# All four block maxima of an attention head as masked maxima on VectorE

## The chip, the core and the metric

The kernel runs on one core of a Trainium2 chip. The metric is the device time of one execution in microseconds (us); before the change its median over three runs is 693.38 us (693.32 to 694.35). A core has five engines with a queue of instructions each, which wait for each other through semaphores: PE (TensorE; its weight loads appear as PEld), DVE (VectorE), ACT (ScalarE), POOL (GpSimd) and SP (SyncE, which issues most DMAs here).

## What is computed

Two independent results are put side by side. B is a 2D real Fourier transform of a 2048 x 576 array, a product with a spectral filter, and the inverse transform. A is attention in four segments of 512 positions with 32 heads of width 18, plus a linear memory that runs on from segment to segment. The change lies in A; cut to what matters:

```python
for s in range(N):                      # N = 4 segments, L = 512
    qs, ks, vs = q[:, :, s], k[:, :, s], v[:, :, s]
    logits = jnp.einsum("bhqd,bhkd->bhqk", qs, ks) * scale + mask   # mask: -1e9 above the diagonal
    p = _softmax(logits, axis=-1)
    a_dot = jnp.einsum("bhqk,bhkd->bhqd", p, vs)
    pq = phi(qs)
    num = jnp.einsum("bhld,bhde->bhle", pq, M)
    den = jnp.einsum("bhld,bhd->bhl", pq, z)[..., None] + 1e-6
    o = g * (num / den) + (1.0 - g) * a_dot
    ...
```

A softmax subtracts each row's maximum before the exponential. The kernel needs those row maxima ahead of the exponentials, and how it gets them is what changes.

## The kernel before

The kernel goes through these stages: the forward transform (to about 65 us), the projections of A with the middle of the transform beside them on VectorE (to about 278 us), the inverse transform with the first eleven heads' maxima between its matmuls (`prologue`, to about 349 us), attention (`attention`, to about 655 us), and the last output projection.

Attention counts heads and segments together: t runs over 128 pairs (segment, head), four of them make a group k. For each t there are two steps, eleven apart. `s1(t+11)` computes the scores with the query on the partitions, only to get the row maxima. `s2(t)` computes the scores again, with the key on the partitions and the maxima taken in as two more rows of the contraction, and ScalarE takes the exponential (L737, L742, L746). The product with the values (`pv`, L768) runs for two heads out of four, two blocks of keys at a time, so that it stands in every second t. Which of its instructions comes after which is written out by hand in `attention`: one part of `s1`, one of `s2`, three times over, with the value product ahead of the third; no scheduler reorders it.

The 512 queries of a head are four blocks of 128, numbered i = 0 to 3. Block i sees 128(i+1) keys, and only its last 128 keys touch the diagonal. `s1` makes three score tiles from one pool with three buffers (`ps1`, tag `s1`), which therefore go round once per head (a fourth kind of tile, the transposed maxima `mt`, takes one turn in every fourth head):

- the first tile holds block 2 (384 columns) and block 0 (128 columns). PE writes the scores (L687) and then adds, with a matmul of the identity `idb` on the triangle `tri` (L700), a large negative number above the diagonal. VectorE takes the maxima of the tile's four 128-wide pieces with a plain reduction (L701) into `mx`.
- the second holds block 3 (512 columns), the third block 1 (256 columns). VectorE adds the mask from `s.mask` and takes the maximum in one instruction, the masked maximum (L695, CUSTOM_DVE in the profile); an accumulator read (DVE_READ_ACCUMULATOR2) stores the result in `mg`. The masked scores themselves are discarded into `junk`, one buffer.
- for t = 11 to 14, the first heads of `attention`, the second and third tile also get the triangle on PE (L691) and a plain reduction (L692).

After four heads `mpath(k)` puts the maxima together: VectorE reduces the three pieces of block 2 (L713), ScalarE copies block 0 (L714), GpSimd splits the values in two bf16 parts (L716, L717), PE transposes them (L720), and a DMA writes them into the two extra rows of the queries.

From about 453 to 492 us and from 537 to 580 us the memory part of a segment (`combine` and `mem1`) runs between the heads, and in the stretches behind them its output projection (`oproj`, L916).

Of the kernel before, what the change touches and what calls it, by code (L numbers as in the profile page):

```python
# [5 lines left out]
F32=mybir.dt.float32; F32R=mybir.dt.float32r  # L6
# [81 lines left out]
class Pace:  # L88

    def __init__(s,total): s.left=total; s.acc=0.0; s.q=[]  # L90
# [275 lines left out]
BF=mybir.dt.bfloat16  # L366
# [43 lines left out]
class ATT:  # L410
    def __init__(s,nc,tc,io,cp,dp):
        s.nc,s.tc,s.io=nc,tc,io
        s.ident=cp.tile([128,128],F32,name="ident"); s.bm=cp.tile([126,7,19],F32,name="bm")
        s.tri=cp.tile([128,128],BF,name="tri"); s.idb=cp.tile([128,128],BF,name="idb")
        s.Mst=[None]+[cp.tile([126,5,126],F32,name=f"Mst{i}") for i in range(1,4)]
        s.zst=[None]+[cp.tile([126,5,32],F32,name=f"zst{i}") for i in range(1,4)]
        d=lambda n,sh,dt: dp.tile(sh,dt,name=n)
        s.qkD=[d(f"qkD{i}",[8,4,128,512],BF) for i in range(4)]
        s.reD=[d(f"reD{i}",[24,32,512],BF) for i in range(4)]
        s.pqD=[None]+[d(f"pqD{i}",[576,512],F32) for i in range(1,4)]  # L420
        s.vD=[d(f"vD{i}",[128,2448],F32) for i in range(4)]
        s.dp=dp
# [203 lines left out]
        return s.stack_dmas(0,0)+s.stack_dmas(0,1)  # L626
    def masks(s):
        nc=s.nc
        nc.scalar.copy(s.tri,s.mask[:,384:])
        nc.scalar.copy(s.idb,s.ident)  # L630
    def gates(s):
        nc=s.nc; e=s.bt
# [47 lines left out]
    def s1(s,t):  # L680

        nc=s.nc; k,hh=divmod(t,4); n,qd=divmod(k,2); h=4*qd+hh
        Q,K=s.Qs[n%3],s.Ks[n%4]; tp=s.sm
        assert (n,0) in s.loaded and (n,1) in s.loaded,(t,n)
        if hh==0: s.mg[k]=tp.tile([128,4,4],F32,name="mg"); s.mx[k]=tp.tile([128,4,4],F32,name="mx")
        def mm(out,i):
            nc.tensor.matmul(out,Q[:108,h,128*i:128*i+128],K[:108,h,:128*(i+1)],start=True,stop=True)  # L687
        def red(src,i):
            w=128*(i+1)
            if 11<=t<15:  # L690
                nc.tensor.matmul(src[:,w-128:w],s.idb,s.tri,start=False,stop=True,skip_group_check=True)  # L691
                nc.vector.tensor_reduce(out=s.mg[k][:,hh,i:i+1],in_=src,axis=mybir.AxisListType.X,op=OP.max)  # L692
                return
            junk=tp.tile([128,512],BF,name="junk",bufs=1)
            nc.vector.tensor_tensor_reduce(out=junk[:,:w],in0=src,in1=s.mask[:,512-w:],scale=1.0,scalar=-3.0e38,  # L695
                op0=OP.add,op1=OP.max,accum_out=s.mg[k][:,hh,i:i+1])
        pa=s.ps1.tile([128,512],F32,name="s1",tag="s1")
        for o,w,i in ((0,384,2),(384,128,0)):
            mm(pa[:,o:o+w],i)
            nc.tensor.matmul(pa[:,o+w-128:o+w],s.idb,s.tri,start=False,stop=True,skip_group_check=True)  # L700
        nc.vector.tensor_reduce(out=s.mx[k][:,hh],in_=pa.rearrange("p (b c) -> p b c",c=128),axis=mybir.AxisListType.X,op=OP.max)  # L701
        yield
        pc=s.ps1.tile([128,512],F32,name="s1",tag="s1")
        mm(pc,3); red(pc,3)
        yield
        pb=s.ps1.tile([128,256],F32,name="s1",tag="s1")
        mm(pb,1); red(pb,1)
        yield
    def mpath(s,k):

        nc=s.nc; n,qd=divmod(k,2); Q=s.Qs[n%3]
        mx=s.mx.pop(k); mg=s.mg.pop(k)
        nc.vector.tensor_reduce(out=mg[:,:,2:3],in_=mx[:,:,:3],axis=mybir.AxisListType.X,op=OP.max)  # L713
        nc.scalar.copy(mg[:,:,0:1],mx[:,:,3:])  # L714
        mh=s.mh; mg=mg.rearrange("p h i -> p (h i)")
        nc.gpsimd.tensor_copy(mh[:,0],mg)  # L716
        nc.gpsimd.tensor_tensor(mh[:,1],mg,mh[:,0],op=OP.subtract)  # L717
        yield
        pt=s.psm.tile([128,1024],BF,name="mt",tag=s.mtag)[:,:128]
        nc.tensor.transpose(pt,mh.rearrange("p a m -> p (a m)"),s.idb)  # L720
        yield
        mt=s.sm.tile([32,128],BF,name="mts",bufs=2)
        nc.scalar.copy(mt,pt[:32])
        out=Q[108:110,4*qd:4*qd+4].rearrange("p h (i c) -> p (h i) c",c=128)
        if s.now<0: nc.gpsimd.dma_start(out,mt)
        else: s.later(2,lambda: nc.scalar.dma_start(out,mt))
        yield
# [226 lines left out]
    def begin(s,sm,sp,ps1):  # L954
        s.late=[]; s.now=-1
        s.sm,s.sp,s.ps1=sm,sp,ps1
        s.mh=sm.tile([128,8,16],BF,name="mh",bufs=1); s.nc.gpsimd.memset(s.mh,0.0)
        s.mg={};s.mx={};s.m2={};s.P={};s.vs={};s.rc={};s.am={};s.pq={};s.ux={};s.rate=1.2;s.potag=s.rest=None
    def prologue(s):

        nc,io=s.nc,s.io
        yield
        s.load_v(0)
        q=s.stack_dmas(1,0)+s.stack_dmas(1,1)+s.stack_dmas(2,0)+s.stack_dmas(2,1)+[lambda: s.load_v(1)]+s.stack_dmas(3,1)
        for i in range(2): yield
        i=0
        for t in range(11):
            for _ in s.s1(t):
                for _ in range(1+(i%24==0)):
                    if q: q.pop(0)()  # L970
                i+=1
                yield
            if 2<=t<6: nc.gpsimd.dma_start(s.Ks[t-2][108:110].rearrange("p h c -> p (h c)"),io["neg1"])
            if t in (3,7): m=s.mpath(t//4); next(m)
            if t in (4,8): next(m); next(m,None)
        assert not q
# [221 lines left out]
```

## Time and profile before

| | |
|---|---|
| median of the runs | 693.38 us |
| lowest and highest of three | 693.32, 694.35 us |
| span of the profiled execution | 692.4 us |
| instructions in it | 14400 |
| granted TensorE clock | 9 tenths or more in all 40 slices |
| HBM read and written | 81.78 MB, 43.92 MB |
| masked maxima on VectorE (L695) | 248, 136.7 us busy |
| plain reductions (L701) | 128, 87.5 us busy |

The profile is one execution. Its span is 1.0 us below the median of the runs. A row of the timeline gives start, duration, engine, line, operation, what it writes and reads, and in brackets the idle time of the engine ahead of it with what ended it. Durations of neighbours on one engine overlap, since an instruction's time runs to its last write and the next one starts earlier; so what an instruction costs its engine is the distance from its start to the next start. The ends of matmuls are modelled. In the queries' names `x` and `x_...` stand for a buffer that is used in turn for several things (the first queries, the first keys and the mask lie in one).

### The profile page before, as it was taken

The numbers are of one execution on the slowest core, as the hardware profiler recorded it, in microseconds if no ns is written. First come the engines' busy times: TensorE is split into PE (matmuls) and PEld (weight loads), VectorE is DVE, ScalarE is ACT, GpSimd is POOL, SyncE is SP. The second block draws the span as 40 slices with busy tenths as digits, with TensorE's granted clock in tenths as the row PEclk, the third lists the DMA queues.
The fourth block names the chain that finished last, engine by engine and source line by source line (L and its number), as shares of the span: only waits on it lengthen the run. The fifth ranks groups of instructions, "written<-read, shape, count | busy, mean of one in ns | idle before, by whom it ended". The sixth has DMA issues, their size and how long they took to land.

```text
span 692.4 us, 14400 instructions
## 1 busy us (share of the span) xinstructions
PE 680.0 (98%) x5040; PEld 502.4 (73%) x5040; DVE 538.0 (78%) x1149; ACT 444.8 (64%) x997; POOL 191.6 (28%) x389
## 2 busy tenths in 40 slices
PE   9999999999999999999999999999999999999997
PEld 5999779879879879899955555445566455673497
DVE  5998989889789679688678888887755877557633
ACT  3876795675684483544468877787756877567531
POOL 2111000100200102656225433434323563235310
PEclk9999999999999999999999999999999999999999
DMA  9896475595486679798337775775756566322152
GB/s 340 288 306 187 141 199 186 172 297 175 145 241 191 196 206 323 187 296 243 100 106 193 203 206 156 202 198 135 162 160 174 151 173 164 122 81 97 28 167 78
DMA packets 76034, 127.60 MB, mean 184 GB/s; under 512 B 12812, under 2 KB 44202, under 8 KB 72370
## 3 DMA queue, kind: packets, MB, share of 16 engines
q1 hardware_dynamic: 69310, 110.67, 54.8%
q0 software_dynamic: 5632, 15.76, 7.9%
q8 instruction: 40, 0.66, 0.4%
q10 hardware_dynamic: 1020, 0.25, 0.2%
q14 instruction: 32, 0.26, 0.1%
HBM read 81.78 MB, written 43.92 MB: 182 GB/s over the span
## 4 chain that ended last, share of the span: by engine, by line
PE 87%; DMA 3%; ACT 3%; DVE 3%; issue 2%; POOL 1%; SPq 0%; ACTq 0%; DVEq 0%; POOLq 0%
PE pj L487 14%; PE pv L768 11%; PE s L687 11%; PE pjv L487 7%; PE po L916 7%; PE i L331 4%; PE i L320 4%; PE s L736 4%; PE f L145 4%; PE c L166 4%; PE s L740 3%; PE s L700 2%; PE po L945 2%; PE pn L843 2%; PE s L745 2%
## 5 line engine op out<-in xcount | busy, mean ns | idle before, releaser
L695 DVE CUSTOM_DVE_ANT_0 junk<-s,x 128x512 bf16<-128x512 f32 x248 | 136.7, 551 | 52.8 <-PE s L687 47.3
L750 POOL TENSOR_SCALAR_AFFINE_SELECT P<-P 128x512 f32<-128x512 f32 (+2 forms) x132 | 79.0, 623 | 71.2 <-ACT P L737 69.5
L701 DVE TENSOR_REDUCE mx<-s 128x4 f32<-128x512 f32 x128 | 87.5, 683 | 2.6 <-PE s L700 0.3
L768 PE MATMUL pv<-P,vs 128*32 128x512 f32 (+3 forms) x1024 | 82.2, 439 | 0.2 <-POOL P L750 0.2
L737 ACT ACTIVATE P<-s 128x512 f32<-128x512 f32 x128 | 77.7, 607 | 7.0 <-PE s L736 4.3
L742 ACT ACTIVATE P<-s 128x512 f32<-128x512 f32 x128 | 77.5, 605 | 2.6 <-PE s L741 2.3
L746 ACT ACTIVATE P<-s 128x256 f32<-128x256 f32 x128 | 49.9, 390 | 44.1 <-PE s L745 43.8
L687 PE MATMUL s<-Ks,Qs 108*128 108x384 bf16 (+3 forms) x256 | 69.2, 301 | 1.5 <-DMA vs<-vD 1.0
L768 PEld LDWEIGHTS pv<-P,vs 128*32 128x32 f32 x1024 | 26.8, 109 | 45.2 <-issue 35.5
L487 PE MATMUL pj<-x,wqkh 128*128 128x512 f32 x162 | 56.1, 408 | 0.0
L232 DVE TENSOR_TENSOR Z<-Z 128x580 f32<-128x580 f32 (+2 forms) x51 | 45.8, 912 | 0.6
L687 PEld LDWEIGHTS <-Qs 108*128 108x128 bf16 x320 | 31.5, 98 | 17.3 <-issue 7.1
L700 PE MATMUL s<-tri,idb 128*128 128x128 bf16 x256 | 43.0, 219 | 0.0
L548 POOL MEMSET vt<- 128x32 f32 x16 | 2.3, 162 | 139.2 <-PE pm L559 79.2
L320 PE MATMUL i<-civ,Y 128*128 128x256 f32 (+1 forms) x288 | 39.6, 289 | 0.9 <-POOL Y L305 0.9
L320 PEld LDWEIGHTS i<-civ,Y 128*128 128x128 f32 (+1 forms) x288 | 36.7, 181 | 1.9 <-POOL Y L305 1.3
L331 PE MATMUL i<-itab,T 128*128 128x290 f32 (+1 forms) x224 | 36.6, 306 | 0.1
L487 PE MATMUL pj<-xh,wqkl 128*128 128x512 f32 x90 | 35.6, 395 | 0.0
L487 PE MATMUL pj<-x,wqkl 128*128 128x512 f32 x90 | 35.5, 395 | 0.0
L487 PE MATMUL pj<-xh,wqkh 128*128 128x512 f32 x90 | 35.5, 395 | 0.0
L487 PEld LDWEIGHTS pj<-x,wqkh 128*128 128x128 f32 x162 | 30.5, 189 | 6.4
L687 PE MATMUL s<-Ks,x 108*128 108x384 bf16 (+3 forms) x128 | 34.6, 300 | 0.2
(216 smaller groups left out, 1792.5 us busy)
## 6 DMA issues: line engine op xcount, KB each, us to landing
qkD<-sp SPq DMA_DIRECT2D x32, 384.0 KB
xin<-xb SPq DMA_DIRECT2D x16, 384.0 KB
cfw<-cfw POOLq DMA_DIRECT2D x16, 384.0 KB, 5.0
civ<-civ POOLq DMA_DIRECT2D x16, 384.0 KB, 8.3
Ks<-qkD SPq DMA_DIRECT2D x12, 512.0 KB
x<-qkD SPq DMA_DIRECT2D x10, 512.0 KB
Qs<-qkD SPq DMA_DIRECT2D x10, 512.0 KB
vs<-vD SPq DMA_DIRECT2D x16, 310.5 KB
```

Source lines behind the costliest of these rows:

```text
L320: nc.tensor.matmul(p[:m,k],Y[i][:,q,c*128:c*128+m],cc[:,hl,o:o+256],start=n==0,stop=n==5)
L331: nc.tensor.matmul(p,x,t,start=n==0,stop=n==6)
L487: s.nc.tensor.matmul(out,a,b,start=i==0,stop=i==len(L)-1)
L687: nc.tensor.matmul(out,Q[:108,h,128*i:128*i+128],K[:108,h,:128*(i+1)],start=True,stop=True)
L695: nc.vector.tensor_tensor_reduce(out=junk[:,:w],in0=src,in1=s.mask[:,512-w:],scale=1.0,scalar=-3.0e38, op0=OP.add,op1=OP.max,accum_out=s.m ...
L700: nc.tensor.matmul(pa[:,o+w-128:o+w],s.idb,s.tri,start=False,stop=True,skip_group_check=True)
L701: nc.vector.tensor_reduce(out=s.mx[k][:,hh],in_=pa.rearrange("p (b c) -> p b c",c=128),axis=mybir.AxisListType.X,op=OP.max)
L737: nc.scalar.activation(P[0][:,hh],p0,AF.Exp,scale=SC)
L742: nc.scalar.activation(P[1][:,hh],p1,AF.Exp,scale=SC)
L746: nc.scalar.activation(P[2][:,hh],p2,AF.Exp,scale=SC)
L750: nc.gpsimd.affine_select(out=x[:,r],in_=x[:,r],pattern=[[0,r.stop-r.start],[1,128]],compare_op=OP.is_ge,fill=0.0,base=0,channel_multiplie ...
L768: nc.tensor.matmul(s.pvt[32*hh:32*hh+32,128*j:],vt[:,152*j+19*h:152*j+19*h+32],mv[0][:,hh,mv[1]],start=j==0,stop=j>1,skip_group_check=True)
```

## The change

All four block maxima of all heads become masked maxima on VectorE. The first tile still holds blocks 2 and 0, and now gets two masked maxima, 384 and 128 wide, which go straight into `mg`. The triangle, its matmuls on PE, the plain reductions, `mx`, and the two instructions of `mpath` that took `mx` apart are gone. The discarded scores go to one of two buffers: `junk512` for blocks 2 and 3, `junk256` for blocks 0 and 1, so that they alternate in the order 2, 0, 3, 1. The third tile is given 512 columns like the others and uses 256 of them.

```diff
-        s.tri=cp.tile([128,128],BF,name="tri"); s.idb=cp.tile([128,128],BF,name="idb")
+        s.idb=cp.tile([128,128],BF,name="idb")
...
     def masks(s):
         nc=s.nc
-        nc.scalar.copy(s.tri,s.mask[:,384:])
         nc.scalar.copy(s.idb,s.ident)
...
-        if hh==0: s.mg[k]=tp.tile([128,4,4],F32,name="mg"); s.mx[k]=tp.tile([128,4,4],F32,name="mx")
-        def mm(out,i):
-            nc.tensor.matmul(out,Q[:108,h,128*i:128*i+128],K[:108,h,:128*(i+1)],start=True,stop=True)
-        def red(src,i):
-            w=128*(i+1)
-            if 11<=t<15:
-                nc.tensor.matmul(src[:,w-128:w],s.idb,s.tri,start=False,stop=True,skip_group_check=True)
-                nc.vector.tensor_reduce(out=s.mg[k][:,hh,i:i+1],in_=src,axis=mybir.AxisListType.X,op=OP.max)
-                return
-            junk=tp.tile([128,512],BF,name="junk",bufs=1)
-            nc.vector.tensor_tensor_reduce(out=junk[:,:w],in0=src,in1=s.mask[:,512-w:],scale=1.0,scalar=-3.0e38,
-                op0=OP.add,op1=OP.max,accum_out=s.mg[k][:,hh,i:i+1])
-        pa=s.ps1.tile([128,512],F32,name="s1",tag="s1")
-        for o,w,i in ((0,384,2),(384,128,0)):
-            mm(pa[:,o:o+w],i)
-            nc.tensor.matmul(pa[:,o+w-128:o+w],s.idb,s.tri,start=False,stop=True,skip_group_check=True)
-        nc.vector.tensor_reduce(out=s.mx[k][:,hh],in_=pa.rearrange("p (b c) -> p b c",c=128),axis=mybir.AxisListType.X,op=OP.max)
-        yield
-        pc=s.ps1.tile([128,512],F32,name="s1",tag="s1")
-        mm(pc,3); red(pc,3)
-        yield
-        pb=s.ps1.tile([128,256],F32,name="s1",tag="s1")
-        mm(pb,1); red(pb,1)
-        yield
+        if hh==0: s.mg[k]=tp.tile([128,4,4],F32,name="mg")
+        def part(*J):
+            p=s.ps1.tile([128,512],F32,name="s1",tag="s1")
+            for o,i in J: nc.tensor.matmul(p[:,o:o+128*i+128],Q[:108,h,128*i:128*i+128],K[:108,h,:128*(i+1)],start=True,stop=True)
+            for o,i in J:
+                w=128*(i+1); b=256*(1+i//2); junk=tp.tile([128,b],BF,name=f"junk{b}",bufs=1)
+                nc.vector.tensor_tensor_reduce(out=junk[:,:w],in0=p[:,o:o+w],in1=s.mask[:,512-w:],scale=1.0,scalar=-3.0e38,
+                    op0=OP.add,op1=OP.max,accum_out=s.mg[k][:,hh,i:i+1])
+        part((0,2),(384,0))
+        yield
+        part((0,3))
+        yield
+        part((0,1))
+        yield
     def mpath(s,k):
 
         nc=s.nc; n,qd=divmod(k,2); Q=s.Qs[n%3]
-        mx=s.mx.pop(k); mg=s.mg.pop(k)
-        nc.vector.tensor_reduce(out=mg[:,:,2:3],in_=mx[:,:,:3],axis=mybir.AxisListType.X,op=OP.max)
-        nc.scalar.copy(mg[:,:,0:1],mx[:,:,3:])
-        mh=s.mh; mg=mg.rearrange("p h i -> p (h i)")
+        mh=s.mh; mg=s.mg.pop(k).rearrange("p h i -> p (h i)")
         nc.gpsimd.tensor_copy(mh[:,0],mg)
```

The order of instructions shows where they stand. On PE, in the head t = 19 of plain attention (the one whose times the prediction reads), from the third score tile of the head before to this head's first `s2` matmul, before the change; s_4550 is that third tile, s_4564 the head's first tile, Qs and Ks the queries and keys:

```order
L687 MATMUL s_4550<-Ks_3172,Qs_3170 128x256 [waits DVE_49]
L745 LDWEIGHTS x_2635
L745 MATMUL s_4554<-x_2635 128x256 [waits Activation_49]
L687 LDWEIGHTS Qs_3170
L687 MATMUL s_4564<-Ks_3172,Qs_3170 128x384 [waits DVE_49]
L700 LDWEIGHTS idb
L700 MATMUL s_4564<-tri,idb 128x128
L687 MATMUL s_4564<-Ks_3172,Qs_3170 128x128
L736 MATMUL s_4573<-Qs_3169,Ks_3171 128x512 [waits Activation_49]
```

And with the change, at the same place (s_4554 is now the third tile of the head before, s_4568 the first tile):

```order
L687 MATMUL s_4554<-Ks_3170,Qs_3168 128x256 [waits DVE_49]
L731 LDWEIGHTS x_2634
L731 MATMUL s_4558<-x_2634 128x256 [waits Activation_49]
L687 LDWEIGHTS Qs_3168
L687 MATMUL s_4568<-Ks_3170,Qs_3168 128x384 [waits DVE_49]
L687 MATMUL s_4568<-Ks_3170,Qs_3168 128x128
L722 MATMUL s_4578<-Qs_3167,Ks_3169 128x512 [waits Activation_49]
```

Four instructions are gone between the first tile and the `s2` matmul, two matmuls and two weight loads (the second pair, behind the 128-wide matmul, reads like the first). What the remaining ones wait for is the same: the first tile's matmul still waits for VectorE to give its buffer free.

On VectorE at the same place, from the masked maximum of the third tile of the head before to the end of this head, before the change (ISA is the masked maximum, and the row behind it, with mg alone, its accumulator read):

```order
L695 ISA junk,mg<-s_4550,x_2635 128x256 [waits DVE_49,PE_49]
L695 ISA mg 128x1
L701 TENSOR_REDUCE mx<-s_4564 128x4 [waits PE_49]
L695 ISA junk,mg<-s_4576,x_2635 128x512 [waits DVE_49,PE_49]
L695 ISA mg 128x1
L695 ISA junk,mg<-s_4585,x_2635 128x256 [waits DVE_49,PE_49]
L695 ISA mg 128x1
L713 TENSOR_REDUCE mg<-mx 128x4
```

And with the change, where junk_4556, junk_4573 and junk_4592 are the smaller buffer and junk_4571 and junk_4583 the larger:

```order
L690 ISA junk_4556,mg<-s_4554,x_2634 128x256 [waits DVE_49,PE_49]
L690 ISA mg 128x1
L690 ISA junk_4571,mg<-s_4568,x_2634 128x384 [waits DVE_49,PE_49]
L690 ISA mg 128x1
L690 ISA junk_4573,mg<-s_4568,x_2634 128x128 [waits DVE_49]
L690 ISA mg 128x1
L690 ISA junk_4583,mg<-s_4581,x_2634 128x512 [waits DVE_49,PE_49]
L690 ISA mg 128x1
L690 ISA junk_4592,mg<-s_4590,x_2634 128x256 [waits DVE_49,PE_49]
L690 ISA mg 128x1
```

In the place of one reduction stand two masked maxima with their reads. The 128-wide one has no wait of its own for PE, so the 384-wide one ahead of it waits for both matmuls of the tile. Each masked maximum still waits for VectorE itself (DVE_49), for the one before the last that wrote the same buffer; before the change the 256-wide one waited for the instruction right in front of it.

More of the change, by code (lines that the diff above doesn't have):

```diff
@@ L957, in begin @@
         s.mh=sm.tile([128,8,16],BF,name="mh",bufs=1); s.nc.gpsimd.memset(s.mh,0.0)
-        s.mg={};s.mx={};s.m2={};s.P={};s.vs={};s.rc={};s.am={};s.pq={};s.ux={};s.rate=1.2;s.potag=s.rest=None
+        s.mg={};s.P={};s.vs={};s.rc={};s.am={};s.pq={};s.ux={};s.rate=1.2;s.potag=s.rest=None
     def prologue(s):
```

## The prediction

> **What bounds the kernel now.** I read the engine line first, then the chain of work that ended last, then the timeline of two neighbouring heads, because a change to both TensorE (PE) and VectorE (DVE) is decided by which of the two the other waits for.
>
> ```profile
> PE 680.0 (98%) x5040; PEld 502.4 (73%) x5040; DVE 538.0 (78%) x1149; ACT 444.8 (64%) x997; POOL 191.6 (28%) x389
> PE 87%; DMA 3%; ACT 3%; DVE 3%; issue 2%; POOL 1%; SPq 0%; ACTq 0%; DVEq 0%; POOLq 0%
> L700 PE MATMUL s<-tri,idb 128*128 128x128 bf16 x256 | 43.0, 219 | 0.0
> ```
>
> These three lines say "PE is the bound; take 256 triangle matmuls off it and gain". That reading needs a check: a matmul's 219 ns runs beyond the start of the next one, and a PE that is held for a fraction of its pipeline still reads as busy. So here is the timeline of PE from the last score tile of one head (call it X, the head behind whose middle tile a value product L768 stands) through the next head (Y) to the head after it:
>
> ```profile
> 364.65 0.28 PE L687 MATMUL s<-Ks,Qs 108*128 108x256 bf16 x1
> 364.77 0.27 PE L745 MATMUL s<-x 110*128 110x256 bf16 x1
> 364.89 0.33 PE L687 MATMUL s<-Ks,Qs 108*128 108x384 bf16 x1
> 365.05 0.22 PE L700 MATMUL s<-tri,idb 128*128 128x128 bf16 x1
> 365.11 0.22 PE L687 MATMUL s<-Ks,Qs 108*128 108x128 bf16 x1
> 365.17 0.22 PE L700 MATMUL s<-tri,idb 128*128 128x128 bf16 x1
> 365.23 0.38 PE L736 MATMUL s<-Qs,Ks 110*128 110x512 bf16 x1
> ...
> 366.00 0.27 PE L745 MATMUL s<-Qs,Ks 110*128 110x256 bf16 x1
> 366.17 0.32 PE L687 MATMUL s<-Ks,Qs 108*128 108x384 bf16 x1
> ...
> 366.77 0.38 PE L687 MATMUL s<-Ks,Qs 108*128 108x512 bf16 x1
> ```
>
> And VectorE in the same stretch:
>
> ```profile
> 364.97 0.42 DVE L695 CUSTOM_DVE_ANT_0 junk<-s,x 128x256 bf16<-128x256 f32 x1 [0.33 <-PE s L687]
> 365.32 0.08 DVE L695 DVE_READ_ACCUMULATOR2_ANT mg<- 128x1 f32 x1
> 365.43 0.69 DVE L701 TENSOR_REDUCE mx<-s 128x4 f32<-128x512 f32 x1
> 366.03 0.68 DVE L695 CUSTOM_DVE_ANT_0 junk<-s,x 128x512 bf16<-128x512 f32 x1
> 366.64 0.08 DVE L695 DVE_READ_ACCUMULATOR2_ANT mg<- 128x1 f32 x1
> 366.87 0.42 DVE L695 CUSTOM_DVE_ANT_0 junk<-s,x 128x256 bf16<-128x256 f32 x1
> 367.21 0.08 DVE L695 DVE_READ_ACCUMULATOR2_ANT mg<- 128x1 f32 x1
> 367.21 0.16 DVE L713 TENSOR_REDUCE mg<-mx 128x4 f32<-128x12 f32 x1
> ```
>
> Two things are to be seen. A triangle matmul delays the next matmul by 0.06 us (365.05 to 365.11, 365.17 to 365.23), not by 0.22. And the 384-wide matmul at 366.17 comes 0.17 after its predecessor, where the same step at 364.77 takes 0.12: it starts 0.05 after the end of L701 (365.43 + 0.69 = 366.12), whose tile it will overwrite. The 512-wide one at 366.77 starts 0.05 after the end of the accumulator read (366.64 + 0.08 = 366.72), for the same reason. The three score tiles go round in three buffers, so here PE already waits for VectorE, once per pair of heads. The closed loop is: PE's 256-wide tile of X (364.65), the masked max on it (364.97), the maxima of Y, the release, the first tiles of the next X, then a fixed run of PE to its 256-wide tile. The triangle matmuls lie in that loop only as far as VectorE waits for them.
>
> **The change, step by step.** PE loses two matmuls a head, 2 x 0.058 = 0.116 us; over 128 heads, with the eight of L691, that is 264 x 0.058 = 15.3 us. This is the gain wherever PE alone sets the pace.
>
> VectorE's costs go by distance between starts. The 512-wide masked max takes 0.61 to its read (366.03 to 366.64), the 256-wide 0.35 (364.97 to 365.32): about 1.0 ns a column, so 384 columns are worked out at 0.47 and 128 at 0.21. Together they are 0.68 in place of the 0.60 of the plain reduction L701 (365.43 to 366.03): 0.08 more a head. Their bounds are the 0.35 row from below and the 0.61 row from above for 384 columns; and for 128 columns the 0.08 of a read and the 0.35 row. I take the line through the two rows, since both forms are the same instruction.
>
> Against that, the 256-wide max now starts 0.23 after the read before it (366.64 to 366.87), although its matmul stood ready: both write the one discarded buffer. With two buffers in turn each masked max waits for the read two back. That is 0.02 late at one place (the 512-wide max: read of the 384-wide at 0.47, plus 0.23, against 0.47 + 0.21) and hidden by the running max at the others. So VectorE's own work per head goes from 0.60 + 0.61 + 0.23 + 0.35 = 1.79 to 0.47 + 0.21 + 0.02 + 0.61 + 0.35 = 1.66.
>
> ```profile
> L713 DVE TENSOR_REDUCE mg<-mx x32: 154/161/164, 307.9 to 629.9; 128x4 f32<-128x12 f32 x32
> L714 ACT COPY mg<-mx x32: 189/218/240, 306.8 to 629.0; 128x4 f32<-128x4 f32 x32
> ```
>
> These two go as well, 32 times each. They stand behind Y's last tile, where VectorE has 0.33 us to spare before X's 256-wide tile (the row at 364.97), so I cost them at nothing; uncovered, they would be worth 32 x 0.08 = 2.6 us at most (L713 held the next start by 0.08 in its pair). The one copy that made the triangle is set-up, beside the projections: nothing.
>
> How many heads stand in which stage shows in the triangle matmuls by stretch, two to a head; the columns are stretch, its length, PE busy (count), weight loads, clock, DMA share, GB/s:
>
> ```profile
> 287.00:345.00 58.00, 3.71 (x22) 2.19 (x22) 1.00 0.84 220
> 358.00:453.00 95.00, 15.78 (x94) 9.13 (x94) 1.00 0.68 183
> 453.00:492.00 39.00, 5.37 (x32) 3.13 (x32) 1.00 0.64 169
> 492.00:537.00 45.00, 5.04 (x30) 2.93 (x30) 1.00 0.58 155
> 537.00:580.00 43.00, 6.05 (x36) 3.52 (x36) 1.00 0.67 178
> 580.00:624.00 44.00, 4.70 (x28) 2.73 (x28) 1.00 0.33 97
> ```
>
> *Beside the inverse transform (11 heads).* The chain there is PE alone, and VectorE waits in every round:
>
> ```profile
> by line: PE i L320 48.4%; PE i L331 36.5%; PE s L687 14.1%; PE s L700 2.1%
> 305.71 0.69 DVE L352 TENSOR_TENSOR T<-i,T 128x512 fp32r<-128x512 f32 x1 [0.48 <-ACT T L350]
> ```
>
> The extra 0.08 on VectorE fits into that 0.48, so 11 x 0.116 = 1.3 us are won.
>
> *Plain attention (47 heads, 23 pairs).* I walk the loop again, from X's 256-wide matmul at 0: max at 0.32, its read at 0.67. Y's second matmul now starts at 0.40 (0.46 less one triangle); VectorE saw the last triangle 0.26 after its start (365.17 to 365.43), so Y's 384-wide max can start at 0.67; 128-wide at 1.14, read at 1.35, and 0.13 later (read 0.08, release 0.05) PE may start its next tile: 1.48, against 366.17 - 364.65 = 1.52. PE itself would be there at 1.24. The 512-wide max starts at 1.37, its read at 1.98, and PE's 512-wide matmul at 2.11, against 2.12. The two triangles leave PE and the wait for VectorE takes their place: 0.01 to 0.02 a pair, 0.3 us. Twice a reciprocal stands in VectorE's way:
>
> ```profile
> 437.70 0.95 DVE L794 RECIPROCAL ry<-ry 128x128 f32<-128x128 f32 x1
> ```
>
> There VectorE is busy without a pause, and its shorter work, 0.13 a head over two or three heads, gives another 0.3.
>
> *Attention with the memory part (34 heads, 17 pairs).* VectorE has one more 512-wide operation a head:
>
> ```profile
> 454.69 0.68 DVE L701 TENSOR_REDUCE mx<-s 128x4 f32<-128x512 f32 x1
> 455.90 0.08 DVE L695 DVE_READ_ACCUMULATOR2_ANT mg<- 128x1 f32 x1
> 455.90 0.68 DVE L895 TENSOR_TENSOR am<-ux,pb 126x512 f32<-126x512 f32 x1
> ```
>
> ```profile
> 455.10 0.27 PE L745 MATMUL s<-x,Ks 110*128 110x256 bf16 x1
> 455.43 0.32 PE L687 MATMUL s<-x,Qs 108*128 108x384 bf16 x1
> ```
>
> L701 ends at 455.37 and PE starts at 455.43, 0.33 after its predecessor: bound by VectorE. Here L895 already stands between read and next max, so no buffer wait goes, and no wait for a triangle: the loop gets 0.10 longer (0.08 of work, 0.02 of wait). If all 17 pairs were like that, 1.7 us would be lost; if none, 34 x 0.116 = 3.9 won. Both kinds stand in these stretches; I take the middle, 1.1 won.
>
> *Attention with the output projection (29 heads).* VectorE waits long for PE:
>
> ```profile
> 498.03 0.42 DVE L695 CUSTOM_DVE_ANT_0 junk<-s,x 128x256 bf16<-128x256 f32 x1 [1.80 <-PE s L687]
> ```
>
> So 29 x 0.116 = 3.4, less 0.2 for the heads at the edges: 3.2 us.
>
> The start of attention (345 to 358, five heads, VectorE against PE) I leave at 0, and behind 632 us nothing is changed. **Sum:** 1.3 + 0.3 + 0.3 + 1.1 + 3.2 = 6.2 us. The span of 692.4 becomes 686.2; the median of the runs lies 1.0 above that span, so 693.4 - 6.2 = 687.2 us.
>
> **The rivals.** *The whole 15.3 us comes, 678.1 us.* For it: the engine shares. Against: the two 0.05 distances above, which say that PE's next tile is VectorE's to give. It needs the release to come 0.24 earlier (1.48 to 1.24), that is, the two short maxima in 0.44 instead of 0.68: both at the cheap ends of their bounds, 0.35 and 0.08.
>
> *The wait behind a read is the accumulator's, not the buffer's; slower.* Every masked max would then start later than the read before it. No row shows a masked max behind a read without the shared buffer, so this stays open: the row at 367.21 (L713 starts with the read) speaks for 0, the read's own duration is 0.08, the row at 366.87 gives 0.23. The loop holds three such places. At 0.08 it gets about 0.2 longer in 23 pairs (5 us), and of the memory part's pairs about half, 0.3 each (2.5 us, in place of the 1.1 won): 693.4 + 5 + 2.5 - 1.3 - 3.2 = 696.4 us. At 0.23 VectorE needs 2 x (1.64 + 4 x 0.23) = 5.1 us a pair against 95.0/23.5 = 4.0 now in the plain part (23 x 1.1 us), 6.3 against 39.0/8 = 4.9 in the memory part (17 x 1.4), and beside the inverse transform 0.5 a head beyond what fits (11 x 0.5): some 55 us more, 748. From about 0.06 on the change loses. I take 0, the nearest row in kind.
>
> A rule of the Trainium skill speaks for this rival: the page "VectorE: DVE Perf Modes", sections "The DRAIN you can't avoid" and "Rules for kernel authors", has the next operation wait for the pipe to empty with or without a semaphore, and advises fewer operations rather than fewer semaphores. By it the two buffers buy nothing and the fourth operation costs, towards the 748. The trace does not agree: 0.23 with the wait on the buffer, 0.00 to L713 without one.
>
> *Nothing measurable, 693.4.* The memory part loses its 1.7 and the plain loop gets 0.12 a pair longer (23 x 0.12 = 2.8, the 128-wide max at 0.33 instead of 0.21), which eats the 1.3 + 3.2.
>
> **How the numbers follow.** Forecast 0.70; the whole gain 0.08; the accumulator's wait 0.17 (0.14 of it clearly slower); nothing 0.05. A measurement of this kernel can tell about 0.2% (1.4 us) from no change. Faster is 0.70 + 0.08 less 0.01: 0.77; same 0.08; slower 0.15. The range runs from 681 (the unknown terms at their better ends: 2.8 more in the memory part, and 3 in the plain part with the 128-wide max at the 0.08 of a read, 23 x 0.13) to 696.5 (the accumulator's wait at the read's duration), leaving out the whole gain and the larger waits.
>
> **What would show it.** In the changed kernel a 128-wide masked max starts 0.47 after a 384-wide one and with its read; the 256-wide one follows the read of the 512-wide at once where its matmul is ready; in plain attention PE's 384-wide matmul still starts 0.05 behind a VectorE end, and a pair still takes about what it takes now; with the output projection a pair is 0.23 shorter. I am wrong if masked maxima start 0.08 or more behind their reads, or if no wait on VectorE is left in the plain part.

## The result, and the profile after

The changed kernel takes 689.3 us, the median of four runs (688.73 to 689.61), against 693.62 us before (four runs, 693.32 to 694.35). The ratio is 0.993 with a 95% interval of 0.9918 to 0.9942: 4.3 us faster. The forecast was 687.2 us, with a range from 681 to 696.5. The span of the profiled execution is 687.8 us.

From the page of the changed kernel come the busy times, the chain's shares by engine, and the masked maxima's group (busy time, mean ns of one, then the idle time ahead of them):

```profile
PE 671.8 (98%) x4776; PEld 486.7 (71%) x4776; DVE 543.0 (79%) x1509; ACT 440.4 (64%) x964; POOL 192.1 (28%) x389
PE 84%; DVE 5%; ACT 3%; DMA 3%; issue 3%; POOL 1%; SPq 0%; ACTq 0%; DVEq 0%; POOLq 0%
L690 DVE CUSTOM_DVE_ANT_0 junk<-s,x 128x384 bf16<-128x384 f32 (+3 forms) x512 | 222.7, 487 | 48.1 <-PE s L687 47.2
```

PE has 264 matmuls less and is still 98% busy; the chain shows what the busy share hides: PE's part of it falls from 87% to 84%, VectorE's rises from 3% to 5%. Three things in the same two heads answer to the timelines of before. First PE, from the 256-wide tile of one head X to the middle tile of the next X:

```profile
363.26 0.28 PE L687 MATMUL s<-Ks,Qs 108*128 108x256 bf16 x1
363.38 0.28 PE L731 MATMUL s<-x 110*128 110x256 bf16 x1
363.49 0.38 PE L687 MATMUL s<-Ks,Qs 108*128 108x384 bf16 x2
363.71 0.38 PE L722 MATMUL s<-Qs,Ks 110*128 110x512 bf16 x1
...
364.48 0.27 PE L731 MATMUL s<-Qs,Ks 110*128 110x256 bf16 x1
364.76 0.38 PE L687 MATMUL s<-Ks,Qs 108*128 108x384 bf16 x2
365.10 0.38 PE L722 MATMUL s<-Qs,Ks 110*128 110x512 bf16 x1
365.39 0.38 PE L687 MATMUL s<-Ks,Qs 108*128 108x512 bf16 x1
...
367.13 0.28 PE L687 MATMUL s<-Ks,Qs 108*128 108x256 bf16 x1
```

And VectorE beside it:

```profile
363.58 0.42 DVE L690 CUSTOM_DVE_ANT_0 junk<-s,x 128x256 bf16<-128x256 f32 x1 [0.45 <-PE s L687]
363.93 0.08 DVE L690 DVE_READ_ACCUMULATOR2_ANT mg<- 128x1 f32 x1
363.93 0.55 DVE L690 CUSTOM_DVE_ANT_0 junk<-s,x 128x384 bf16<-128x384 f32 x1
364.41 0.08 DVE L690 DVE_READ_ACCUMULATOR2_ANT mg<- 128x1 f32 x1
364.41 0.29 DVE L690 CUSTOM_DVE_ANT_0 junk<-s,x 128x128 bf16<-128x128 f32 x1
364.62 0.08 DVE L690 DVE_READ_ACCUMULATOR2_ANT mg<- 128x1 f32 x1
364.63 0.69 DVE L690 CUSTOM_DVE_ANT_0 junk<-s,x 128x512 bf16<-128x512 f32 x1
365.25 0.08 DVE L690 DVE_READ_ACCUMULATOR2_ANT mg<- 128x1 f32 x1
365.25 0.42 DVE L690 CUSTOM_DVE_ANT_0 junk<-s,x 128x256 bf16<-128x256 f32 x1
```

A masked maximum starts with the read before it (363.93, 364.41, 365.25), or 0.01 to 0.02 behind it where it is the 512-wide one (364.63; 0.02 in 41 of the 46 heads of the plain part): the accumulator's wait, the slower rival, is not there. The 384-wide one takes 0.48 to its read and the 128-wide one 0.21. On PE the triangles are gone (the `x2` at 363.49 is the first tile's two matmuls), and the 384-wide matmul at 364.76 comes 0.28 behind its predecessor where it came 0.17 behind: it starts 0.06 after the read at 364.62 has ended (364.70). The 512-wide one at 365.39 starts 0.06 after the end of the next read (365.33). The pair takes 367.13 - 363.26 = 3.87 us. Before, the corresponding pair began at 364.65 and ended here:

```profile
368.52 0.28 PE L687 MATMUL s<-Ks,Qs 108*128 108x256 bf16 x1
```

That is 3.87 us too. In this pair the wait for VectorE took the place of the triangles to the hundredth.

Stage by stage, from the starts of score matmuls L687 in the two traces (the 384-wide one of t = 0 and 11, the 256-wide one of t = 16, 62, 79, 93, 111, 125; the plain part is t = 16 to 62):

| stage | before | after | difference | forecast |
|---|---|---|---|---|
| ahead of t = 0 | 287.78 | 287.45 | -0.33 | 0 |
| beside the inverse transform | 62.12 | 60.83 | -1.29 | -1.3 |
| start of attention | 10.83 | 11.07 | +0.24 | 0 |
| plain | 92.81 | 92.31 | -0.50 | -0.6 |
| memory part, twice | 84.07 | 83.29 | -0.78 | -1.1 |
| output projection, twice | 86.13 | 83.96 | -2.17 | -3.2 |
| behind t = 125 | 68.66 | 68.93 | +0.27 | 0 |

The first and last rows hold next to nothing that the change touches and show how far two executions differ there. The largest miss is the output projection. There the changed kernel has a wait that the sum did not, first on PE, then on VectorE:

```profile
495.27 0.28 PE L687 MATMUL s<-Ks,Qs 108*128 108x256 bf16 x1
495.39 0.22 PE L706 MATMUL mt<-idb,mh 128*128 128x128 bf16 x1
...
495.78 0.38 PE L722 MATMUL s<-Qs,x 110*128 110x512 bf16 x1
496.08 0.38 PE L687 MATMUL s<-Ks,Qs 108*128 108x512 bf16 x1
```

```profile
495.94 0.08 DVE L690 DVE_READ_ACCUMULATOR2_ANT mg<- 128x1 f32 x1
```

The middle tile comes 0.30 behind its predecessor instead of 0.22. The transposed maxima `mt` have taken a turn of the three buffers at 495.39, so the tile at 496.08 is the third turn after the 256-wide one of 495.27 and needs its buffer: it starts 0.06 after the end of that tile's read (495.94 + 0.08 = 496.02). Over both stretches PE's starts on this wait and its like are late by 0.94 us in all (a start counts as late beyond the distance that its predecessor's width takes elsewhere, 0.22 us for 512 columns), against 0.03 before. This is most of the missing 1.0 us.

### The profile page after: what moved, and what is told of

The parts are those of the page before. It is cut to its first block, busy times and chain, and to the rows that moved or that the text cites. A ratio compares the mean times of both kernels' runs of the same rounds, so it can differ in the third digit from the quotient of the medians.

```text
span 687.8 us, 14313 instructions
## 1 busy us (share of the span) xinstructions
PE 671.8 (98%) x4776; PEld 486.7 (71%) x4776; DVE 543.0 (79%) x1509; ACT 440.4 (64%) x964; POOL 192.1 (28%) x389
## 4 chain that ended last, share of the span: by engine, by line
PE 84%; DVE 5%; ACT 3%; DMA 3%; issue 3%; POOL 1%; SPq 0%; ACTq 0%; DVEq 0%; POOLq 0%
PE pj L487 15%; PE pv L754 11%; PE s L687 11%; PE pjv L487 7%; PE po L902 7%; PE i L331 4%; PE i L320 4%; PE f L145 4%; PE c L166 4%; PE s L722 3%; PE s L726 3%; PE po L931 2%; PE pn L829 2%; DVE junk L690 2%; PE pm L559 2%
## 5 line engine op out<-in xcount | busy, mean ns | idle before, releaser
L690 DVE CUSTOM_DVE_ANT_0 junk<-s,x 128x384 bf16<-128x384 f32 (+3 forms) x512 | 222.7, 487 | 48.1 <-PE s L687 47.2
L687 PE MATMUL s<-Ks,Qs 108*128 108x384 bf16 (+3 forms) x256 | 65.2, 300 | 3.0 <-DVE mg L690 2.3
L687 PEld LDWEIGHTS <-Qs 108*128 108x128 bf16 x320 | 31.2, 98 | 19.2 <-issue 12.4
L690 DVE DVE_READ_ACCUMULATOR2_ANT mg<- 128x1 f32 x512 | 42.5, 83 | 0.0
L506 DVE SCALAR_TENSOR_TENSOR ex<-pj,ex 128x512 f32<-128x512 f32 (+1 forms) x28 | 19.3, 689 | 19.5 <-ACT ex L504 19.4
L687 PE MATMUL s<-Ks,x 108*128 108x384 bf16 (+3 forms) x128 | 32.7, 299 | 0.6 <-ACT mts L709 0.2
```

What stands on the lines that cost most here:

```text
L687: for o,i in J: nc.tensor.matmul(p[:,o:o+128*i+128],Q[:108,h,128*i:128*i+128],K[:108,h,:128*(i+1)],start=True,stop=True)
L690: nc.vector.tensor_tensor_reduce(out=junk[:,:w],in0=p[:,o:o+w],in1=s.mask[:,512-w:],scale=1.0,scalar=-3.0e38, op0=OP.add,op1=OP.max,accum_ ...
```

## The experiments

Each kernel is timed beside the kernel before on the same chip; the kernel before took 693.5 to 693.8 us there.

### The triangles and the reductions apart

Only the triangle matmuls are taken out of the kernel before:

```diff
-            nc.tensor.matmul(pa[:,o+w-128:o+w],s.idb,s.tri,start=False,stop=True,skip_group_check=True)
...
-                nc.tensor.matmul(src[:,w-128:w],s.idb,s.tri,start=False,stop=True,skip_group_check=True)
```

> The kernel before, with the triangle matmuls left out (L700 and L691; the maxima of blocks 2 and 0, and of all blocks in four heads, are then taken without the mask) and VectorE's plain reduction kept. Theory (a loop of PE and VectorE over two neighbouring heads sets the pace of plain attention, PE alone that of the heads beside the inverse transform and beside the output projection): VectorE no longer waits for the last triangle, so a plain pair gets 0.11 us shorter (23 pairs, 2.7 us); inverse transform 1.3, output projection 2.8, memory part 2.0; together about 8.8, 684.8 us. Rival 1 (PE sets the pace everywhere): 15.3 less, 678.3 us. Rival 2 (VectorE's work per head sets the pace everywhere): within 1 us of 693.6.

Measured: 686.45 us, ratio 0.9896 (0.9879 to 0.9912), 7.1 us won. The plain part of its trace is only 0.17 us shorter (92.81 to 92.64), but this execution is the longest of the four (689.05 us; the others took 686.0 to 686.65), and for 3.4 us of its plain part the granted clock was 0.50. The row gives the stretch, its length, the busy times of PE, PEld, DVE, ACT and POOL, the granted clock, and the share and rate of the DMAs:

```profile
436.40:439.80 3.40, 3.40 (x22) 0.90 (x19) 1.96 (x8) 1.68 (x4) 2.19 (x6) 0.50 0.77 220
```

A value product stands in it, and takes 2.24 us to the next matmul, where another in the same trace takes 1.21:

```profile
384.56 1.28 PE L766 MATMUL pv<-P,vs 128*32 128x384 f32 x16
385.77 0.28 PE L687 MATMUL s<-Ks,x 108*128 108x256 bf16 x1
...
437.67 2.31 PE L766 MATMUL pv<-P,vs 128*32 128x512 f32 x16
439.91 0.28 PE L687 MATMUL s<-Ks,Qs 108*128 108x256 bf16 x1
```

The pair of heads around it took 6.90 us, against 5.43 before. The other 22 pairs took 85.74 us against 87.38, 1.64 less: every second pair is 0.11 shorter (3.81 against 3.92), as the theory had it for each, and those between, all but one, are 0.01 shorter at most (3.86 against 3.87). With VectorE as it was and PE freed, PE's starts in 54 us ahead of that stretch are late by 2.2 us for VectorE and 1.9 us for ScalarE, where the kernel before has 1.6 and 0.2.

Next, only the two buffers for the discarded scores, in the kernel before:

```diff
-            junk=tp.tile([128,512],BF,name="junk",bufs=1)
+            b=256*(1+i//2); junk=tp.tile([128,b],BF,name=f"junk{b}",bufs=1)
```

> The kernel before, with the discarded scores in two buffers by size and nothing else changed. Theory: the wait of the 256-wide maximum for the read before it (0.23 us, 124 times) goes, but it stands where VectorE has time to spare in the loop; only where a reciprocal fills VectorE does it show: 0.3 to 0.5 less, 693.2 us. Rival (VectorE's work per head sets the pace): up to 124 x 0.14 = 17 us less, 676 us.

Measured: 693.51 us, ratio 1.0001 (0.9991 to 1.001). The plain part is 0.6 us shorter and the start of attention 0.3 longer. The 0.23 us that VectorE no longer waits is worth next to nothing in the whole kernel.

Then the triangles put back into the changed kernel, so that PE does the old work and VectorE the new:

```diff
+            for o,i in J:
+                if i in (0,2): nc.tensor.matmul(p[:,o+128*i:o+128*i+128],s.idb,s.tri,start=False,stop=True,skip_group_check=True)
```

> The changed kernel with the triangle matmuls put back on PE (the mask is then added twice in blocks 2 and 0, which changes no maximum). Theory: the 384-wide maximum waits for the last triangle again, a plain pair gets 0.10 longer (23 pairs, 2.3 us), and PE's own 0.116 a head comes back beside the inverse transform (1.3), the output projection (2.2) and in part of the memory pairs (1.0): 689.3 + 6.8 = 696.1 us. Rival (PE sets the pace everywhere): 689.3 + 15.3 = 704.6 us. Rival 2 (VectorE's work alone sets the pace): 689.3 us.

Measured: 698.93 us, ratio 1.008 (1.0065 to 1.0095), 2.8 us above the theory. With the first kernel of this section it gives both halves of the change in both surroundings: the triangles cost 693.5 - 686.45 = 7.1 us with the plain reductions and 698.9 - 689.3 = 9.6 us with the masked maxima; VectorE's side of the change costs 698.9 - 693.5 = 5.4 us with the triangles and 689.3 - 686.45 = 2.85 us without. The theory's 0.10 a pair came out as 0.11 in most pairs. The excess over it lies in the plain part (3.55 us instead of 2.3) and the memory part (1.85 instead of 1.0) above all; it is partly a pause of 0.46 us on PE at the first tile with newly loaded queries and keys, every eighth head of the plain part; why it is there was not found.

### One discarded buffer in the changed kernel

```diff
-                w=128*(i+1); b=256*(1+i//2); junk=tp.tile([128,b],BF,name=f"junk{b}",bufs=1)
+                w=128*(i+1); b=512; junk=tp.tile([128,b],BF,name=f"junk{b}",bufs=1)
```

> The changed kernel with one discarded buffer for all four masked maxima. Theory: each masked maximum then starts about 0.23 us after the read before it, VectorE needs 5.1 us a pair instead of 3.3 and sets the pace of the plain and the memory part: about 55 us more, 744 us, with the rows of the trace showing 0.23 from every read to the next start. Rival (the read itself holds the next maximum back whatever the buffer): as the changed kernel, 689.3 us.

Measured: 732.59 us, ratio 1.0559 (1.0543 to 1.0575): 43.3 us slower than the changed kernel. VectorE's timeline in the plain part:

```profile
380.63 0.08 DVE L690 DVE_READ_ACCUMULATOR2_ANT mg<- 128x1 f32 x1
380.74 0.29 DVE L690 CUSTOM_DVE_ANT_0 junk<-s,x 128x128 bf16<-128x128 f32 x1
380.96 0.08 DVE L690 DVE_READ_ACCUMULATOR2_ANT mg<- 128x1 f32 x1
381.19 0.69 DVE L690 CUSTOM_DVE_ANT_0 junk<-s,x 128x512 bf16<-128x512 f32 x1
381.80 0.08 DVE L690 DVE_READ_ACCUMULATOR2_ANT mg<- 128x1 f32 x1
382.03 0.42 DVE L690 CUSTOM_DVE_ANT_0 junk<-s,x 128x256 bf16<-128x256 f32 x1
```

Now every maximum starts behind its read, by 0.11 (380.74) or 0.23 (381.19, 382.03). The plain part grew by 24.2 us, the memory part by 11.4 and the start of attention by 5.1, while the output projection, where VectorE waits for PE, grew by 1.6 only, and the part beside the inverse transform by 0.01. In the traced execution the granted clock was 0.50 in three stretches of 3.4 us (from 354.0, 360.9 and 463.3 us), two of them in the start of attention and one in the plain part, so some of the growth of these two stages is the clock's; outside them the plain pairs took 4.93 to 4.96 us where the changed kernel's take 3.87 to 3.92. So the wait belongs to the shared buffer and not to the accumulator, and the second buffer, worth nothing in the kernel before, is what the change cannot do without. The estimate of 744 was right for the plain part (23 x 1.1 = 25.3 us) and too high in the memory part (17 x 1.4 = 23.8, against 11.4), where VectorE's other operations stand behind some of the reads without a pause, as the prediction had seen at L895, which may be why, and beside the inverse transform (11 x 0.5 = 5.5), where PE alone sets the pace.

### Three score buffers or four

In heads 16 to 61 one bank of the accumulator memory (`post`) is idle, but for a single tile at about 415 us. Every fourth score tile is put there:

```diff
-            p=s.ps1.tile([128,512],F32,name="s1",tag="s1")
+            s.n4=s.n4+1 if 16<=t<62 else 0
+            p=s.ps.tile([128,512],F32,name="s1",tag="post") if s.n4%4==3 else s.ps1.tile([128,512],F32,name="s1",tag="s1")
```

> The changed kernel, with every fourth score tile of the heads 16 to 61 (plain attention) in the PSUM bank that stands idle there, so that four buffers go round instead of three; no instruction more or less. Theory (PE waits for VectorE's release of the tile three back): the waits of 0.23 to 0.35 us a pair in the plain part go, about 20 pairs: 4 to 6 less, 684.8 us. Rival (the distance between neighbouring tiles is set by something else, ScalarE's exponentials or PE's own queue): 689.3 us.

Measured: 685.9 us (685.39 to 687.34), ratio 0.9889 (0.9875 to 0.9904), 3.4 us better than the changed kernel; the best of all that were run that leave nothing out. The plain part goes from 92.31 to 89.06 us, all other stages stay within 0.7. In 52 us of it PE no longer waits for VectorE's releases (4.1 us in 55 of the changed kernel) but for ScalarE, 2.4 us instead of 0.9. Of this kernel, ScalarE's timeline, then PE's:

```profile
385.33 0.58 ACT L761 COPY U<-pv 128x512 f32<-128x512 f32 x1
385.80 0.61 ACT L724 ACTIVATE P<-s 128x512 f32<-128x512 f32 x1
```

```profile
385.95 0.38 PE L688 MATMUL s<-x,Qs 108*128 108x384 bf16 x2
386.46 0.38 PE L723 MATMUL s<-Qs,Ks 110*128 110x512 bf16 x1
```

The matmul at 386.46 is 0.29 late (0.51 behind its predecessor's start, where the two matmuls take 0.22): it waits for the exponential at 385.80, which ends at 386.41 and stands behind the copy of the value product.

The same fourth buffer in the kernel before, on all three tiles:

> The kernel before (triangles and plain reductions kept), with every fourth score tile of heads 16 to 61 in the idle post buffer. Theory (before the change PE waits for VectorE's releases only about 0.11 us a pair of heads, so a fourth buffer gives 23 x 0.11 = 2.5 us here and the triangles then hold PE everywhere): 691.0 us. Its plain part (92.8 us before) then takes about 90.3, against 89.1 in the changed kernel with the fourth buffer, so that ScalarE's waits leave 1.2 of the 46 x 0.116 = 5.3 us of triangles. Rival (the fourth buffer is worth as much here as in the changed kernel, 3.4 us, since the buffers bound both alike): 690.1. Rival (the buffers hold nothing while the triangles are there): 693.5.

Measured: 692.73 us, ratio 0.9985 (0.9976 to 0.9994), 0.8 us won, less than either theory that expected a gain. PE's waits for VectorE are gone there too, but its waits for ScalarE grow to 0.9 us in 54. The four kernels side by side:

| | three score buffers | four |
|---|---|---|
| before the change: time, plain part | 693.6, 92.81 | 692.7, 91.85 |
| after: time, plain part | 689.3, 92.31 | 685.9, 89.06 |

The change is worth 4.3 us with three buffers and 6.8 with four, and the plain part, where it gave 0.50 us, gives 2.79. So what swallowed the triangles there is the return of the score buffers. Of the 46 x 0.116 = 5.3 us that 46 heads' triangles held PE, 2.5 stay missing with four buffers. There PE waits for ScalarE: over the whole plain part its starts are late for ScalarE by 4.6 us in the changed kernel with four buffers and by 2.2 in the kernel before with four, 2.4 more.

That was tried as well: with four buffers, the copy of the value product on VectorE in the plain part.

```diff
-        (s.nc.vector.tensor_copy if s.now>=117 else s.nc.scalar.copy)(s.U[:,qd],s.pvt)
+        (s.nc.vector.tensor_copy if s.now>=117 or s.now<51 else s.nc.scalar.copy)(s.U[:,qd],s.pvt)
```

> The changed kernel with the fourth buffer in heads 16 to 61, and there the copy of the value product out of its PSUM buffer (0.5 to 0.6 us, once in four heads) on VectorE in place of ScalarE. Theory (with the fourth buffer ScalarE is the bound in the plain part, 2.4 us of PE's waits in 55, while VectorE has 0.4 us idle in places): 11 copies x 0.3 to 0.47 us: 682 to 683 us, against 685.9 without it. Rival (VectorE is as full: 4 x 1.64 + 0.61 = 7.17 us of work in four heads that take 7.2, so the wait only changes its engine): 685.5 to 687. Rival (the copy stands ahead of maxima on VectorE and holds the score buffers): 689 or more.

Measured: 687.71 us, ratio 0.9915 (0.99 to 0.993), no gain and probably a loss of some 1.8 us. Of this kernel VectorE, then PE:

```profile
385.55 0.69 DVE L761 COPY U<-pv 128x512 f32<-128x512 f32 x1
386.15 0.55 DVE L691 CUSTOM_DVE_ANT_0 junk<-s,x 128x384 bf16<-128x384 f32 x1
```

```profile
386.45 0.38 PE L723 MATMUL s<-Qs,Ks 110*128 110x512 bf16 x1
386.97 0.38 PE L688 MATMUL s<-x,Qs 108*128 108x512 bf16 x1
```

The copy holds VectorE for 0.60 us, and the middle tile at 386.97 is 0.30 late. PE's waits for ScalarE fall from 2.4 us to less than 0.2 and those for VectorE rise from nothing to 2.4: the wait changes its engine. Neither of the two engines has room for this copy there.

### Two attempts at the loop that missed, and one that shows little

The value product in three visits in four heads instead of two, so that each pause of the scores is shorter:

```diff
-for j in ((0,3),(),(1,2),())[jj]:
+for j in ((0,),(3,2),(1,),())[jj]:
```

> The changed kernel, with the value product of a group spread over three heads (one key block, two, one) instead of two heads with two blocks each; the same matmuls. Theory: VectorE then falls behind in one head of four instead of two, a group of the plain part gets about 0.4 us shorter (11.5 groups, 4.5 us), one of the memory part 0.2 (1.7), and the third visit costs PE about 0.2 a group beside the output projection (1.4): 684.5 us. Rival (PE sets the pace): the third visit's cost alone, 32 x 0.2 = 6 more, 695 us.

Measured: 692.79 us, ratio 0.9988 (0.9979 to 0.9997), 3.5 us slower than the changed kernel and not 4.8 faster. PE's timeline shows the three visits of a group and what comes behind each:

```profile
381.29 1.06 PE L754 MATMUL pv<-P,vs 128*32 128x512 f32 x8
382.28 0.28 PE L687 MATMUL s<-Ks,x 108*128 108x256 bf16 x1
...
383.62 0.86 PE L754 MATMUL pv<-P,vs 128*32 128x128 f32 x16
384.41 0.28 PE L687 MATMUL s<-Ks,x 108*128 108x256 bf16 x1
...
385.61 0.85 PE L754 MATMUL pv<-P,vs 128*32 128x384 f32 x8
386.39 0.28 PE L687 MATMUL s<-Ks,x 108*128 108x256 bf16 x1
```

They take 0.99 + 0.79 + 0.78 = 2.56 us, where two visits of the changed kernel (365.91 to 367.13 is one, 1.22) take 2.44, and each visit's first matmul is late by another 0.09. A group of four heads thus costs PE 0.21 us more. In the plain part shorter waits for VectorE paid for that (92.66 against 92.31 us); in the stages behind it, where there is little to be won, the 16 groups cost 3.4 us by this sum and 4.1 as measured.

The transposed maxima in the free half of the third score tile, so that they take no turn:

```diff
+            if J[0][1]==1: s.p3=p
...
-        pt=s.psm.tile([128,1024],BF,name="mt",tag=s.mtag)[:,:128]
+        pt=s.psm.tile([128,1024],BF,name="mt",tag=s.mtag)[:,:128] if s.mtag=="mt" else s.p3[:,256:320].bitcast(BF)
```

> The changed kernel, with the transposed maxima in the free half of the third score tile instead of in a turn of their own in the ring of three. Theory: the second tile behind the transposition no longer waits for the 256-wide maximum (0.08 us, once a group): 7 groups beside the output projection and some of the others, 0.6 to 1.5 less, 688.2 us. Rival: 689.3 us or, as the third tile is now held by ScalarE's copy too, up to 1 us more.

Measured: 708.92 us, ratio 1.0216 (1.0199 to 1.0233). VectorE, then PE:

```profile
377.43 0.08 DVE L691 DVE_READ_ACCUMULATOR2_ANT mg<- 128x1 f32 x1
```

```profile
377.56 0.22 PE L707 MATMUL s<-idb,mh 128*128 128x128 bf16 x1 [0.52 <-DVE mg L691]
```

The transposition now shares a tile with a maximum that VectorE is still to take, and holds PE's queue until that is done, 0.69 us each time: a wait was removed from the middle tile and a longer one put ahead of it. Three edits at once (the fourth buffer, three visits, this one) have the same fault:

> The changed kernel with the fourth buffer, the three visits and the maxima off the ring together. Theory: the first two take away the same waits in the plain part, so their gains there do not add: fourth buffer 4.5, three visits 1.7 in the memory part against 1.4 beside the output projection and 1 to 2 of their own cost in the plain part, maxima 1.0: 683 to 686 us. Rival (PE sets the pace): above 690 us.

Measured: 711.26 us, ratio 1.0253 (1.0238 to 1.0268).

With the transposed maxima in the idle bank, where they share no tile, in heads 16 to 61:

```diff
-        pt=s.psm.tile([128,1024],BF,name="mt",tag=s.mtag)[:,:128]
+        q,m=(s.ps,"post") if 5<=s.now<51 else (s.psm,s.mtag)
+        pt=q.tile([128,1024],BF,name="mt",tag=m)[:,:128]
```

> The changed kernel with three score buffers, and in heads 16 to 61 the transposed maxima in the idle post buffer, so that they take no turn of the score buffers. Theory (the loop of a pair, release of the score buffers by VectorE, sets the pace; the transposition's turn costs only the 0.08 us by which the second tile behind it is late, 11 times): 688.4 us, from 688.2 to 689.3. Rival (the transposition's turn is what the fourth buffer took away): 685.9. Rival (nothing): 689.3.

Measured: 688.93 us, ratio 0.9927 (0.9915 to 0.994), which cannot be told from the changed kernel's 0.993. PE's waits at the middle tile fell from 2.38 to 1.92 us in 55, those at the first tile rose from 1.68 to 2.11: in the plain part the loop through VectorE stands, whichever tile shows it. The fourth buffer's gain is therefore not the transposition's turn. The output projection, where that turn costs, has no idle bank, and it was not tried there.

## Why the prediction was right, and where it was off

The direction and the mechanism held; the gain was 4.3 us instead of 6.2. That the time lies in the range says little, since the range ran from 681 us to 696.5, beyond the time before.

- **Beside the inverse transform**, -1.3 forecast and -1.29 measured: PE alone sets the pace there.
- **VectorE's prices.** The prediction took 0.47 and 0.21 from the line through two widths; the line through 0.35 and 0.61 itself gives 0.48 and 0.22, and 0.48 and 0.21 were measured. The 0.02 lateness of the second buffer showed as 0.01 to 0.02.
- **The plain loop.** The walk put PE's next first tile at 1.48 and its middle tile at 2.11 after X's 256-wide matmul; measured 364.76 - 363.26 = 1.50 and 2.13. So triangles turned into waits for VectorE, and that the cause is the return of the buffers is shown by the fourth buffer. That -0.6 became -0.50 is in part luck. The ordinary pairs kept their 3.92 and 3.87 us, so the 0.01 to 0.02 a pair did not come. The pair with the reciprocal at 437.70 gained 0.23 and one more with short extra work on VectorE 0.06, together the other 0.3; two pairs that the sum had no reason for, those behind t = 38 and 44, gained 0.13 and 0.17, and the last lost 0.08. Two buffers alone, in the kernel before, gained 0.14 behind t = 38 and 0.46 at the reciprocal.
- **The accumulator's wait** (the slower rival) is refuted by the starts at 0.00 and by the one-buffer kernel, where the wait came back and cost 43.3 us. The rule that spoke for it, in the Trainium skill's page "VectorE: DVE Perf Modes", section "Rules for kernel authors", that fewer operations count and not fewer semaphores, does not fit this kernel: the same operations with a wait between neighbours took 732.59 us, without it 689.3. The other section that the prediction names there, "The DRAIN you can't avoid", also says that a next operation which the engine does not hold back starts earlier; the prediction left that out, and the starts at 0.00 agree with it.
- **The whole gain** (678.1) is refuted by the pair times, and no edit came near it: the best version is at 685.9.
- **Nothing measurable** is refuted by the interval of the ratio, 0.9918 to 0.9942, and by the memory part, which won 0.78 us where this rival lost 1.7.
- **The output projection is the mis-sized term**: 3.2 forecast, 2.17 measured. The step "VectorE waits long for PE, so 29 x 0.116" looked at VectorE's wait ahead of the 256-wide maximum, 1.80 us, and not at the buffers' order behind a transposition, where PE without its triangles comes to the middle tile before the buffer is free. The kernel with only the triangles taken out has the same waits (0.27 us at four middle tiles in its second stretch, 0.40 in the changed kernel's), so they come from the freed PE more than from the new maxima.
- **The memory part**, 1.1 forecast as the middle of a loss of 1.7 and a gain of 3.9, gave 0.78; a middle so far from both its ends that comes out this close is partly luck. **The start of attention** was put at 0 and came out at +0.24. It was 0.58 shorter in the kernel with the plain reductions and no triangles, which speaks for VectorE's longer work as the price, but it was 0.3 longer than before with the two buffers alone, where VectorE had no more work. Neither was taken apart further, and the cause at the start of attention stays open.

## What to carry to other kernels

Work taken off a busy engine is worth what lies between its next two waits: walk the closed loop through the buffers and the other engine before multiplying the instruction's cost by its count. Where the walk shows that a buffer's return takes the place of the work, look for an idle buffer in that stage along with the change; here it raised the gain from 4.3 to 7.7 us, and most of PE's waits left in that stage were for the third engine. And where operations that also write a result nobody reads follow each other closely, neighbours should not share the place for it: the same second buffer was worth 0.0 us before the change and 43.3 us after, of which some was the granted clock. Before two traces are compared stage by stage, the granted clock of each stage has to be read: half the clock for 3.4 us hid most of a gain of 1.64 us.

## What was not expected of the hardware

An accumulator read lasts 0.08 us and yet costs VectorE nothing between starts: the next masked maximum begins with it. With one shared buffer the next one starts 0.23 us after the read's start where it also waits for PE, and 0.11 us where it waits for VectorE alone (the 128-wide one); whether the second wait makes that difference was not tested.
